# Column-group sums behind relu in late items, and first-pass evictions ahead of a conversion

## The chip, the cores and the metric

The kernel runs on one core of a Trainium2 chip. The time is the device time of one execution in microseconds (us); the median of three runs of the kernel before is 480.83 us (479.24 to 481.24). Engines as the profile names them: PE is TensorE (PEld its weight loads), DVE is VectorE, ACT is ScalarE, POOL is GpSimd, SP is SyncE, which issues the transfers.

## The reference

Three stages follow each other: chunked attention with memory tokens, a soft mixture of experts, and a squared-relu feed-forward layer. The change lies in the last:

```
h = x @ w_in            # x: 3072 x 512, w_in: 512 x 2048
r = np.maximum(h, 0.0)
g = s * (r * r) + b
out = g @ w_out         # w_out: 2048 x 512
```

Here x is itself `c @ slot_out`, with c of 32 columns (one per slot), so that h = c @ (slot_out @ w_in). The kernel forms m = slot_out @ w_in first, and h from c and m with one matmul for each block.

## The kernel before

The last stage cuts the 3072 tokens into 8 blocks of 384, and the 2048 hidden columns into 16 blocks f of 128. One pair (token block, f) is an **item**. Items 0 to 15 are the first pass: token blocks 0 and 1 in turn, f from 0 to 7. Items 16 to 47 are the second: blocks 2 and 3 in turn, all 16 f. Then blocks 4 to 7 follow alone, and at the end blocks 0 and 1 for f from 8 to 15.

Work of one item n: a matmul of 384 columns into a bank of the PSUM pool "s", which has two banks (`emit_h`, line 825, tile s); on ScalarE relu (line 831), square (line 835) and a rounded copy ghi (line 839); on VectorE the rest glo = square - ghi (line 842). Three items later nine matmuls of 512 columns use them: ghi and glo with the high part of w_out (`emit_o`, line 877) and, an item later still, ghi with its low part (`emit_o2`, line 889). They add up in three banks for each token block: pt, x, xt for one, lp and two of g for the other. When the last f of a run is done, the three sums are scaled and evicted, two on VectorE (line 896), one on ScalarE (line 894). After the first pass, the first matmul of the second pass on the same three banks waits for that. Square has two buffers, so the square of item n needs glo of item n-2 to be done.

The weights arrive packed and are converted on the way, one block in every second item up to item 46: ScalarE scales (`stage_a`, line 579), VectorE takes steps 0 to 3 (`stage_d`: lines 589, 591, 593, 600), and for w_out ScalarE casts a high part (`stage_w`, line 798) and VectorE forms the low part (lines 791, 793). Items 0 to 14 and 32 to 46 convert w_out, items 16 to 30 the later columns of w_in. Packed blocks lie in a ring of three slots; SyncE refills a slot when its last conversion is done (line 212).

The matrix m is made in groups of 512 columns. Group 0 is made around the first items, outside this loop. Groups 1, 2 and 3 are made in items 4, 26 and 34 (`M_AT`), each in two steps: in item n eight matmuls (line 806), which leave partial sums in four groups of 32 partitions, and ScalarE's copy of them to the tile mps (line 808); in item n+1 two matmuls that add the four groups and spread the sum (line 812), ScalarE's copy of the result into mpack (line 817), and VectorE's rest for the lower half (line 818). Both steps take a bank of the pool "s". These are the sums over column groups of which the change speaks.

Nothing schedules the work: each engine runs its instructions in the order in which the loop over n writes them, and waits on semaphores for the others. So where `emit_m` and `emit_m2` stand in the loop sets where lines 808 and 817 stand in ScalarE's queue.

Of the kernel before, what the change touches and what calls it, by code (L numbers as in the profile page):

```python
# [35 lines left out]
def kernel(  # L36
# [30 lines left out]
    def psum(tag, shape):  # L67
        bufs = {"s": 2, "g": 2}.get(tag, 1)
        return ps.tile(shape, F32, tag=tag, name=tag, bufs=bufs)
# [48 lines left out]
    with tc.manual_schedule():  # L118
# [45 lines left out]
        NRG, E_AT = 3, 5  # L164
        EARLY = [("wi", 2), ("wi", 3)]
        order = [("w1", i) for i in range(W1)] + [("wi", 0), ("wi", 1)] + [("w2", i) for i in range(W2)]
# [4 lines left out]
        order = order[0:-E_AT] + EARLY + order[-E_AT:]  # L171
# [9 lines left out]
        last_use = {}  # L181
# [7 lines left out]
        wnext = [0]  # L189
# [382 lines left out]
        def wi_dst(t, key):  # L572
            j = key[2]
            return t[j % 2][:, :, 256 * (j // 2):256 * (j // 2) + 256]
# [6 lines left out]
        def cv_dve(key, j):  # L581
            h, lf, a, w = cv[key]
            H = w[:, :, 1]
            hi, ai = h.bitcast(I32), a.bitcast(I32)
            if key[0] == "i" and key[1] > 1 and j:
                ai = wi_dst(wis_b if key[1] % 2 else wis_a, key).bitcast(I32)
                hi, H = (x.rearrange("p (k f) -> p k f", k=2) for x in (hi, H))
            if j == 0:
                nc.vector.tensor_scalar(out=hi, in0=hi, scalar1=3, scalar2=None, op0=ALU.logical_shift_left)
            elif j == 1:  # L590
                nc.vector.scalar_tensor_tensor(out=ai, in0=H, scalar=SIGN, in1=hi, op0=ALU.bitwise_and, op1=ALU.bitwise_or)
            else:
                nc.vector.tensor_scalar(out=hi, in0=ai, scalar1=EXPM, scalar2=None, op0=ALU.bitwise_and)

        def cv_low(key, out):
            h, lf, a, w = cv[key]
            low = w[:, :, 0].bitcast(U32)
            if key[0] == "i":
                low, h = (x.rearrange("p (k f) -> p k f", k=2) for x in (low, h))
            nc.vector.scalar_tensor_tensor(out=out, in0=low, scalar=2.0 ** -52, in1=h, op0=ALU.mult, op1=ALU.mult)  # L600
# [145 lines left out]
        M_AT = (4, 26, 34)  # L746
# [14 lines left out]
        HF = NF // 2  # L761
# [20 lines left out]
        def stage_d(k, j):  # L782
            key = cq.get(k)
            if key:
                h, lf, a, w = cv[key]
                if j < 3:
                    cv_dve(key, j)
                elif j == 3:
                    cv_low(key, lf if key[0] == "o" else wi_dst([wis_l[:, 0:2], wis_l[:, 2:4]], key))
                elif key[0] == "o" and j == 4:  # L790
                    nc.vector.tensor_tensor(out=a, in0=a, in1=w_hi[key[1]].bitcast(F32), op=ALU.subtract)
                elif key[0] == "o":
                    nc.vector.tensor_tensor(out=w_lo[key[1]], in0=a, in1=lf, op=ALU.add)

        def stage_w(k):
            key = cq.get(k)
            if key and key[0] == "o":
                nc.scalar.copy(out=w_hi[key[1]], in_=cv[key][2])

        def emit_m(fb):  # L800
            wis = wis_b if fb % 2 else wis_a
            mp = psum("s", [128, 512])
            for lo in range(1 if fb == 1 else 2):
                for kc in range(KD):
                    lhsT, rhs = (soTb[:, kc, :], wis_l[:, kc, :]) if lo else (soT4[:, kc, 0, :], wis[kc // 2][:, kc % 2, :])
                    nc.tensor.matmul(out=mp[32 * kc:32 * kc + 32, :], lhsT=lhsT, rhs=rhs,
                                     start=(lo == 0), stop=(lo == 1 or fb == 1))
            nc.scalar.copy(out=mps, in_=mp)

        def emit_m2(fb):  # L810
            mr = psum("s", [128, 512])
            nc.tensor.matmul(out=mr, lhsT=stks_all, rhs=mps, start=True, stop=True)
            m_split(mr, 512 * fb, slice(0, 512))

        def m_split(mp, base, cols):
            m = mpack[:, base + cols.start:base + cols.stop]
            nc.scalar.copy(out=m, in_=mp[:, cols])
            nc.vector.tensor_tensor(out=m[64:128], in0=mp[64:128, cols], in1=m[64:128].bitcast(F32), op=ALU.subtract)  # L818

        def emit_h(n):  # L820
            if n >= len(items):
                return
            (b, _, _), f = items[n]
            hq = psum("s", [128, UT])
            nc.tensor.matmul(out=hq, lhsT=mpack[:, 128 * f:128 * f + 128], rhs=cpack[:, b * UT:(b + 1) * UT],  # L825
                             start=True, stop=True)
            h_t[n] = hq

        def emit_relu(n):
            if n < len(items):  # L830
                nc.scalar.activation(out=r_g[n % 2], in_=h_t.pop(n), func=AF.Relu)  # L831
# [5 lines left out]
        def emit_ghi(n):  # L837
            if n < len(items):
                nc.scalar.copy(out=ghi_g[n % (LA + 2)], in_=r2_g[n % 2])  # L839
# [15 lines left out]
        def store(b, t, os_):  # L855
            nc.sync.dma_start(out=out[b * UT + 128 * t:b * UT + 128 * t + 128, :], in_=os_)

        def os_early(b, t):
            return area(16 * SLOT + DM * (NTU * b + t), DM)
# [20 lines left out]
        def emit_o2(n):  # L880
            r_, f = items[n]
            b, f0, f1 = r_
            ghi, glo = ghi_g[n % (LA + 2)], glo_g[n % (LA + 2)]
            for t in range(NTU):
                o = o_t[r_][t]
                if n == len(items) - 1:
                    for gt in (ghi, glo):
                        nc.tensor.matmul(out=o, lhsT=gt[:, 128 * t:128 * t + 128], rhs=w_hi[f], start=False, stop=False)
                nc.tensor.matmul(out=o, lhsT=ghi[:, 128 * t:128 * t + 128], rhs=w_lo[f], start=False, stop=(f == f1 - 1))  # L889
                if f == f1 - 1:  # L890
                    if b < 4 and f0 == 0:
                        to = part[b][t] if b < 2 else os_early(b - 2, t)
                        if t == 1:
                            nc.scalar.activation(out=to, in_=o, func=AF.Copy, scale=sbt[:, 0:1])
                        else:
                            nc.vector.tensor_scalar(out=to, in0=o, scalar1=sbt[:, 0:1], scalar2=None, op0=ALU.mult)  # L896
                    else:
                        os_ = os_g[t]
                        nc.vector.scalar_tensor_tensor(out=os_, in0=o, scalar=sbt[:, 0:1], in1=part[b][t] if f0 else bias,
                                                       op0=ALU.mult, op1=ALU.add)  # L900
                        store(b, t, os_)
# [12 lines left out]
        def stages(n, *js):  # L914
            for j in js:
                stage_d(n, j)


        cp = (nc.scalar.copy, nc.vector.tensor_copy)
        sot = psum("g", [128, 2, 4, 32])  # L920
# [47 lines left out]
        for n in range(LA + 1, len(items) + LA + 1):  # L968
            if n > 7:
                emit_h(n)  # L970
            m = n - LA - 1
            ends = 0 <= m and items[m][1] == items[m][0][2] - 1
            late = m + 1 < len(items) and m + 1 == 2 * HF + 1
            if ends or late:
                emit_o2(m)
            if 1 < m + 1 < len(items):
                emit_o(m + 1)
            if m > 1 and not ends and not late:
                emit_o2(m)
            if LA + 1 < n <= 7:  # L980
                emit_h(n)
            if n == 6:
                nc.vector.tensor_copy(out=soTb, in_=soT4[:, :, 0, :])
            if n in M_AT:
                emit_m(M_AT.index(n) + 1)
            if n - 1 in M_AT:
                emit_m2(M_AT.index(n - 1) + 1)
            emit_relu(n)
            emit_sq(n)
            stage_a(n + 1)  # L990
            emit_ghi(n)
            if LA + 1 < n <= len(items):
                emit_g(n - 1)
            stage_d(n, 1)
            stage_w(n)
            stages(n, 2, 3)
            stages(n - 1, 4, 5)
            stage_d(n + 1, 0)
            if 48 <= n < 64:
                for i in (2 * n - 96, 2 * n - 95):  # L1000
                    wsum_add(i)
            if n == 64:
                colsum()
            if 65 <= n < 77:
                add_bias(n - 65)
            while wnext[0] < len(order) and last_use.get(order[wnext[0] - NRG], -1) <= n:
                load_w(1)


# [70 lines left out]
```

## Time and profile before

| | us |
|---|---|
| median of three runs | 480.83 (479.24 to 481.24) |
| profiled execution | 479.52 |
| its span | 477.7 |
| PE busy | 456.7 (96%) |
| DVE busy | 310.1 (65%) |
| ACT busy | 308.7 (65%) |
| POOL busy | 84.4 (18%) |
| DMA engines, share of the span (q1) | 44.6% |

Busy times are sums over the span; they say which engine is worked most, not what an edit in one stage is worth. The last stage starts at about 167 us, and the changed items lie between 204 and 290 us. The profile gives each wait by the engine and line that ended it; a matmul's busy time includes its way through the pipeline, so that matmuls in a row overlap in it.

### The profile page before, as it was taken

To read this page: it belongs to the slowest core of one execution; us is meant where nothing else is said; L and a number is where in the kernel's file an instruction comes from. 1 tells how busy PE (TensorE), PEld (TensorE's weight loads), DVE (VectorE), ACT (ScalarE), POOL (GpSimd) and SP (SyncE) were. 2 spreads that over 40 slices of the span, in tenths; PEclk is the share of its full clock that TensorE was granted. 3 is DMA by queue.
4 is the path that set the end of the run, shared out by engine and by line. 5 is a ranking of instruction groups with operands and counts; after the bars stand their busy time and mean duration, and the time that the engine had idled before them with its cause. 6 is when DMAs were issued, how large, how long until landed. Compare 5 with 4: busy or idle time off the path is not lost.

```text
span 477.7 us, 10206 instructions
## 1 busy us (share of the span) xinstructions
PE 456.7 (96%) x3960; PEld 342.3 (72%) x3960; DVE 310.1 (65%) x685; ACT 308.7 (65%) x635; POOL 84.4 (18%) x154
## 2 busy tenths in 40 slices
PE   7899998999999999999898999999999999999996
PEld 5666666665555467868585888888888888888885
DVE  6778887885485889997484999975524224223232
ACT  4566666675144388888576897666666666666660
POOL 6666665650000000000000000007700000000000
PEclk9999999999999999999999999999999999999999
DMA  8999999999999934234222000003101001001011
GB/s 304 385 406 405 406 409 398 397 381 396 401 420 392 414 128 151 89 99 166 88 89 88 1 1 0 1 0 146 55 0 67 0 1 67 0 1 66 1 67 66
DMA packets 20576, 83.04 MB, mean 174 GB/s; under 512 B 2736, under 2 KB 2864, under 8 KB 14640
## 3 DMA queue, kind: packets, MB, share of 16 engines
q1 hardware_dynamic: 20528, 82.39, 44.6%
q8 instruction: 31, 0.51, 0.4%
q14 instruction: 17, 0.14, 0.1%
HBM read 76.09 MB, written 6.29 MB: 172 GB/s over the span
## 4 chain that ended last, share of the span: by engine, by line
PE 69%; DVE 13%; DMA 8%; ACT 4%; issue 3%; SPq 2%; POOL 1%; DVEq 0%; POOLq 0%; ACTq 0%
PE g L877 11%; PE lp L877 5%; PE pt L877 5%; PE x L877 5%; PE g L889 5%; PE xt L877 5%; PE s L825 4%; DMA seg<-in_w_dram 4%; PE s L630 3%; PE x L325 3%; DMA vals<-in_vm_dram 3%; PE lp L889 3%; PE pt L889 3%; PE xt L889 3%; PE x L889 3%
## 5 line engine op out<-in xcount | busy, mean ns | idle before, releaser
L842 DVE TENSOR_TENSOR glo<-r,ghi 128x384 fp32r<-128x384 f32 x128 | 76.3, 601 | 81.6 <-ACT ghi L839 81.4
L831 ACT ACTIVATE r<-s 128x384 f32<-128x384 f32 x128 | 62.8, 491 | 52.8 <-PE s L825 52.4
L835 ACT ACTIVATE r<-r 128x384 f32<-128x384 f32 x128 | 67.4, 527 | 6.2 <-DVE glo L842 2.0
L839 ACT CAST ghi<-r 128x384 fp32r<-128x384 f32 x128 | 65.7, 513 | 3.4
L825 PE MATMUL s<-cpack,mpack 128*128 128x384 f32 x128 | 44.2, 348 | 3.7 <-ACT r L831 2.1
L301 ACT ACTIVATE seg<-seg 128x384 f32<-128x384 f32 x32 | 28.8, 900 | 19.2 <-DVE seg L312 15.1
L889 PE MATMUL g<-wlo,ghi 128*128 128x512 f32 x128 | 40.2, 394 | 0.0
L877 PE MATMUL g<-whi,ghi 128*128 128x512 f32 x126 | 39.7, 394 | 0.2 <-DVE mpack L818 0.2
L877 PE MATMUL g<-whi,glo 128*128 128x512 f32 x126 | 39.3, 393 | 0.0
L864 POOL TENSOR_TENSOR keys<-keys,bias 128x512 f32<-128x512 f32 x6 | 8.4, 1426 | 168.7 <-DVE bias L853 168.7
L263 POOL TENSOR_SCALAR keys<-keys 64x416 f32<-64x416 f32 x63 | 33.7, 536 | 12.7 <-DMA keys<-in_kq_dram 7.5
L285 PE MATMUL s<-keys 128*32 128x128 f32 x768 | 30.3, 291 | 4.4 <-POOL keys L267 3.4
L825 PEld LDWEIGHTS s<-cpack,mpack 128*128 128x128 f32 x128 | 23.9, 188 | 13.0 <-ACT r L831 4.4
L325 PE MATMUL x<-vals,seg 128*32 128x128 f32 x744 | 28.0, 275 | 2.8 <-DMA vals<-in_vm_dram 2.0
L325 PEld LDWEIGHTS x<-vals,seg 128*32 128x32 f32 x744 | 20.3, 109 | 13.2 <-DVE seg L309 6.4
L889 PEld LDWEIGHTS g<-wlo,ghi 128*128 128x128 f32 x128 | 24.0, 188 | 5.3
L877 PEld LDWEIGHTS g<-whi,glo 128*128 128x128 f32 x126 | 23.7, 188 | 5.3
L285 PEld LDWEIGHTS s<-keys 128*32 128x32 f32 x768 | 19.5, 113 | 10.4 <-POOL keys L267 6.0
L319 ACT COPY seg<-pt 128x384 f32<-128x384 f32 x32 | 15.3, 478 | 17.9 <-PE pt L317 16.9
L877 PEld LDWEIGHTS g<-whi,ghi 128*128 128x128 f32 x126 | 23.7, 188 | 4.3 <-DVE mpack L818 0.7
L877 PE MATMUL lp<-whi,ghi 128*128 128x512 f32 x63 | 25.5, 404 | 0.9 <-DVE vals L896 0.9
L877 PE MATMUL pt<-whi,ghi 128*128 128x512 f32 x64 | 25.6, 400 | 0.0
(255 smaller groups left out, 991.1 us busy)
## 6 DMA issues: line engine op xcount, KB each, us to landing
seg<-in_w_dram SPq DMA_DIRECT2D x27, 1024.0 KB, 8.5
keys<-in_kq_dram SPq DMA_DIRECT2D x32, 396.0 KB, 7.4
vals<-in_vm_dram SPq DMA_DIRECT2D x64, 192.0 KB, 6.5
keys<-in_w_in_dram SPq DMA_DIRECT2D x5, 1024.0 KB, 5.1
keys<-in_w_out_dram SPq DMA_DIRECT2D x5, 1024.0 KB, 4.9
out_dram<-os SPq DMA_DIRECT2D x18, 256.0 KB, 2.1
vals<-in_w_in_dram SPq DMA_DIRECT2D x3, 1024.0 KB, 5.6
vals<-in_w_out_dram SPq DMA_DIRECT2D x3, 1024.0 KB, 4.9
```

The costliest lines, as they stand in the source:

```text
L263: (nc.vector if h and u == 0 else nc.gpsimd).tensor_scalar(out=stream(kz[rows, h], 0, CH), in0=k[rows, UT * h:UT * h + (NCU + 1) * CH].rea ...
L285: nc.tensor.matmul(out=o, lhsT=qt[:, 32 * c:32 * c + 32], rhs=kz[:, :, at:at + WIN], start=True, stop=not (first or last))
L301: nc.scalar.activation(out=p_r[u], in_=sm_r[u].rearrange("p t h (a r) -> p t r (h a)", a=2), func=AF.Exp, scale=scale)
L319: nc.scalar.copy(out=pts_r[u], in_=pt)
L325: nc.tensor.matmul(out=xp[32 * r:32 * r + 32, t], lhsT=pts_r[u][:, 32 * c:32 * c + 32], rhs=vbuf[u // 2 % 2][:, u % 2, :, 64 * c:64 * c + ...
L825: nc.tensor.matmul(out=hq, lhsT=mpack[:, 128 * f:128 * f + 128], rhs=cpack[:, b * UT:(b + 1) * UT], start=True, stop=True)
L831: nc.scalar.activation(out=r_g[n % 2], in_=h_t.pop(n), func=AF.Relu)
L835: nc.scalar.activation(out=r2_g[n % 2], in_=r_g[n % 2], func=AF.Square)
L839: nc.scalar.copy(out=ghi_g[n % (LA + 2)], in_=r2_g[n % 2])
L842: nc.vector.tensor_tensor(out=glo_g[n % (LA + 2)], in0=r2_g[n % 2], in1=ghi_g[n % (LA + 2)].bitcast(F32), op=ALU.subtract)
L877: nc.tensor.matmul(out=o_t[r_][t], lhsT=gt[:, 128 * t:128 * t + 128], rhs=w_hi[f], start=(f == r_[1] and gt is ghi), stop=False)
L889: nc.tensor.matmul(out=o, lhsT=ghi[:, 128 * t:128 * t + 128], rhs=w_lo[f], start=False, stop=(f == f1 - 1))
```

## The change

Two edits in the loop over n, and nothing else; no instruction is added or removed.

The two steps of a column group (`sums`) stand ahead of relu only in items up to 7, that is, for group 1. For groups 2 and 3 (items 26, 27, 34 and 35) they stand behind relu, square, the scaling of the next weight block and ghi, still ahead of glo of the item before.

The conversion steps of item 18 (`convert`, from step 1 on) and the refill that depends on them are written in item 19, behind the evictions of item 15 (the second token block of the first pass).

```
+        def sums(n):
+            if n in M_AT:
+                emit_m(M_AT.index(n) + 1)
+            if n - 1 in M_AT:
+                emit_m2(M_AT.index(n - 1) + 1)
+
+        def convert(n):
+            stage_d(n, 1)
+            stage_w(n)
+            stages(n, 2, 3)
+            stages(n - 1, 4, 5)
+            stage_d(n + 1, 0)
...
             if ends or late:
                 emit_o2(m)
+            if n == 2 * HF + 3:
+                convert(n - 1)
             if 1 < m + 1 < len(items):
                 emit_o(m + 1)
...
-            if n in M_AT:
-                emit_m(M_AT.index(n) + 1)
-            if n - 1 in M_AT:
-                emit_m2(M_AT.index(n - 1) + 1)
+            if n <= 7:
+                sums(n)
             emit_relu(n)
             emit_sq(n)
             stage_a(n + 1)
             emit_ghi(n)
+            if n > 7:
+                sums(n)
             if LA + 1 < n <= len(items):
                 emit_g(n - 1)
-            stage_d(n, 1)
-            stage_w(n)
-            stages(n, 2, 3)
-            stages(n - 1, 4, 5)
-            stage_d(n + 1, 0)
+
+            if n != 2 * HF + 2:
+                convert(n)
...
-            while wnext[0] < len(order) and last_use.get(order[wnext[0] - NRG], -1) <= n:
+            while n != 2 * HF + 2 and wnext[0] < len(order) and last_use.get(order[wnext[0] - NRG], -1) <= n:
                 load_w(1)
```

HF is 8, so the two numbers are 18 and 19. On ScalarE, at items 26 and 27 (rows with + are new, with - gone; r and ghi are item 26's, then item 27's):

```order
+L831 ACTIVATE r_2658<-s 128x384
+L835 ACTIVATE r_2660<-r_2658 128x384
+L839 CAST ghi_2663<-r_2660 128x384
 L808 COPY mps_2657<-s 128x512
-L831 ACTIVATE r_2658<-s 128x384
-L835 ACTIVATE r_2660<-r_2658 128x384
-L839 CAST ghi_2663<-r_2660 128x384
+L831 ACTIVATE r_2659<-s 128x384
+L835 ACTIVATE r_2661<-r_2659 128x384
+L579 ACTIVATE seg_99<-keys 128x512
+L839 CAST ghi_2664<-r_2661 128x384
 L817 CAST mpack<-s 128x512
```

The copy to mps now follows item 26's three activations, and the copy into mpack follows item 27's four; at items 34 and 35 it is the same, with one cast of line 798 between the copy to mps and item 35's relu. TensorE's order is the same in both kernels.

On VectorE, at the end of the first pass (glo of item 17, the conversion of item 18, the evictions of item 15, glo of item 18):

```order
 L842 TENSOR_TENSOR glo_2669<-r_2661,ghi_2664 128x384
+L896 TENSOR_SCALAR vals_104<-lp,cstt 128x512
+L896 TENSOR_SCALAR vals_104<-g,cstt 128x512
 L591 SCALAR_TENSOR_TENSOR seg_99<-keys 128x2x256
 L593 TENSOR_SCALAR keys<-seg_99 128x512
 L600 SCALAR_TENSOR_TENSOR seg_101<-keys 128x2x256
-L896 TENSOR_SCALAR vals_104<-lp,cstt 128x512
-L896 TENSOR_SCALAR vals_104<-g,cstt 128x512
 L842 TENSOR_TENSOR glo_2670<-r_2660,ghi_2665 128x384
```

The two evictions now stand ahead of the three conversion steps; glo of item 18 stays behind all five.

## Rows read from the trace of the kernel before

**Rows 1.** Busy time by stretch: us, PE, PEld, DVE, ACT, POOL, PEclk, DMA share, GB/s.

```profile
230.00:240.00 10.00, 8.25 (x40) 5.85 (x33) 5.10 (x9) 7.34 (x16) 0.00 (x0) 1.00 0.31 105
...
260.00:270.00 10.00, 10.00 (x46) 8.29 (x45) 9.79 (x20) 8.76 (x18) 0.00 (x0) 1.00 0.01 2
```

**Rows 2.** Waits from 205 to 330 us: engine, line, releaser; total, times, longest us.

```profile
PE s L825 <- ACT r L831: 2.1, 2, 1.1
...
PE s L825 <- ACT mps L808: 1.4, 2, 0.7
...
PE lp L877 <- DVE vals L896: 0.9, 1, 0.9
...
PEld s L825 <- ACT mps L808: 2.8, 2, 1.4
```

**Rows 3.** Timeline, items 26 to 30: start, us, engine, instruction, [idle before, releaser].

```profile
226.85 0.34 PE L825 MATMUL s<-cpack,mpack 128*128 128x384 f32 x1
...
230.08 0.40 PE L806 MATMUL s<-seg 128*32 128x512 bf16 x4
230.52 0.59 ACT L808 COPY mps<-s 128x512 f32<-128x512 f32 x1 [3.54 <-PE s L806]
...
231.16 0.45 PE L825 MATMUL s<-cpack,mpack 128*128 128x384 f32 x1 [0.68 <-ACT mps L808]
...
233.50 1.02 PE L812 MATMUL s<-mps,stk 128*128 128x512 f32 x2
234.56 0.59 ACT L817 CAST mpack<-s 128x512 fp32r<-128x512 f32 x1 [1.96 <-PE s L812]
...
235.18 0.69 DVE L818 TENSOR_TENSOR mpack<-s,mpack 64x512 fp32r<-64x512 f32 x1 [3.97 <-ACT mpack L817]
...
235.91 0.56 DVE L842 TENSOR_TENSOR glo<-r,ghi 128x384 fp32r<-128x384 f32 x1
...
237.94 0.34 PE L825 MATMUL s<-cpack,mpack 128*128 128x384 f32 x1
...
238.81 0.39 PE L877 MATMUL pt<-whi,glo 128*128 128x512 f32 x1
...
240.20 0.34 PE L825 MATMUL s<-cpack,mpack 128*128 128x384 f32 x1
```

**Rows 4.** Timeline: the hidden-layer matmuls of items 34 and 37.

```profile
249.24 0.34 PE L825 MATMUL s<-cpack,mpack 128*128 128x384 f32 x1
...
260.35 0.34 PE L825 MATMUL s<-cpack,mpack 128*128 128x384 f32 x1
```

**Rows 5.** Timeline at the end of the first pass, items 18 to 21.

```profile
209.65 0.63 PE L889 MATMUL g<-wlo,ghi 128*128 128x512 f32 x2
...
211.28 0.69 DVE L591 SCALAR_TENSOR_TENSOR seg<-keys 128x512 int32<-128x512 int32 x1
...
211.98 0.34 PE L825 MATMUL s<-cpack,mpack 128*128 128x384 f32 x1
...
213.07 0.75 DVE L896 TENSOR_SCALAR vals<-lp,cstt 128x512 f32<-128x512 f32 x1
...
214.38 0.55 DVE L842 TENSOR_TENSOR glo<-r,ghi 128x384 fp32r<-128x384 f32 x1
...
215.56 0.34 PE L825 MATMUL s<-cpack,mpack 128*128 128x384 f32 x1
...
216.43 0.40 PE L877 MATMUL pt<-whi,glo 128*128 128x512 f32 x1
```

**Rows 6.** Timeline: glo of items 36 and 38 on VectorE.

```profile
262.72 0.55 DVE L842 TENSOR_TENSOR glo<-r,ghi 128x384 fp32r<-128x384 f32 x1
...
267.12 0.55 DVE L842 TENSOR_TENSOR glo<-r,ghi 128x384 fp32r<-128x384 f32 x1
```

**Rows 7.** SyncE's issues of w_in (timeline), and time to landing (page part 6).

```profile
204.32 9.22 SPq L212 DMA_DIRECT2D keys<-in_w_in_dram  x2
...
keys<-in_w_in_dram SPq DMA_DIRECT2D x5, 1024.0 KB, 5.1
```

## The prediction

> **What bounds the kernel now.** I read the busy table by stretches first. In most of the last stage TensorE has no idle time (10.00 us of 10 in 260 to 270), while 230 to 240 shows 8.25; its clock is granted in full in both [rows 1]. So the last stage is paced by matmuls except at a few holes, and only a hole can be won. The list of waits names them: twice 0.7 us until ScalarE's copy of the column-group sums (line 808), twice 1.1 us until a relu, and 0.9 us until a VectorE eviction (line 896) [rows 2]. No other wait of a matmul between 205 and 330 us is in that list. Then I read the timeline at each hole, and there the reader sees the queue rather than the work: ScalarE stood idle for 3.54 us before the copy at 230.52, because the copy needs the eight matmuls that end at 230.48, and item 26's relu, whose matmul started at 226.85, stood behind it [rows 3].
>
> **Sums behind ghi, items 26 and 34.** Nothing is added or removed; on ScalarE two copies change places with relu, square and ghi of the same item. The price before, first place: from item 26's hidden-layer matmul at 226.85 to that of item 29 at 237.94 are 11.09 us, against 3 x 2.26 = 6.78 for three steady items (237.94 to 240.20 is one) [rows 3]. After: relu, square and ghi of item 26 fit in the 3.54 us that ScalarE was idle, so item 27's matmul no longer waits for the copy. It starts when the eight matmuls end (230.48; they start the steady item's end, 226.85 + 2.26 = 229.11, so they cost 1.37). Its first successors then run as before, up to the regrouping matmuls 2.34 us later (231.16 to 233.50, less 0.11 for the restart below: 2.23, so 232.71). Their input, the copy, is there: ScalarE is free, and starts it at 230.52 as before, done by 231.11. These two matmuls take 1.02, to 233.73. Item 28's matmul needs item 27's relu, which now stands in front of the second copy: it starts after the first copy, about 231.0, and is done by 231.5. So no hole is left: 6.78 + 1.37 + 1.02 = 9.17, and 11.09 - 9.17 = 1.92. Matmuls that follow without a wait overlap a little (two in a row are busy 0.63 together where one is 0.40 [rows 5]), which adds up to 0.17 at each of the two holes: at most 2.26. The least is the two idle times alone, 0.7 + 1.1 = 1.8 [rows 2]. I take 2.0, near the upper end, since it rests on whole items. The second place has the same length, 249.24 to 260.35 = 11.11 [rows 4], so another 2.0.
>
> What is late next: the second copy starts when the regrouping ends, 233.73 + 0.04, not at 234.56. VectorE's split of it (line 818) keeps its old place, ahead of glo of item 26, and starts 0.62 after the copy: 234.4; glo follows 0.73 later and ends at about 235.7 [rows 3]. TensorE reads that glo at 238.81 before, at 236.8 after: the margin falls from 2.34 to 1.1 us, but stays. Square of item 28 waits for the same glo (they share a buffer), so ScalarE is idle for about a microsecond there; the relu of item 28 is ahead of that and done by 234.8, and item 29's matmul, which now waits for it (it gets its bank), comes at 236.0. So nothing reaches TensorE.
>
> **A restart, weighed with the skill.** The weight load of that matmul waited too, 2.8 us at two places [rows 2], and the matmul after a wait is busy 0.45 us where the steady one takes 0.34 [rows 3]; each hole therefore costs about 0.11 beyond its idle time, and that comes back with it. The Trainium skill (TensorE: Matmul & The Clock Gate, Engine queue depths) says that TensorE's queue can pull a weight load ahead of matmuls in flight. By that rule no restart would be paid, and the sum below would be 0.11 x 5 = about 0.5 us smaller (476.2); the trace shows the load held up along with its matmul, so I keep the row's price.
>
> **Evictions ahead of item 18's conversion.** On VectorE, three conversion steps (lines 591, 593, 600) and two evictions of 128x512 change places. Their sum is unchanged: the steps take 213.07 - 211.28 = 1.79, the evictions 214.38 - 213.07 = 1.31, and glo of item 18 still starts at 214.38 [rows 5]. The evicted sums were complete at 209.65 + 0.63 = 210.28, so the evictions can start at 211.28 and free their banks by 212.7. The items around it are 211.98 to 215.56 = 3.58 apart instead of 2.26: TensorE gets 1.32 at most, and at least the 0.85 to 0.9 of pure idle time [rows 2, 5]. One thing eats into this: glo of item 18 ends at 214.93 as before, and TensorE, now 1.32 earlier, wants it at 215.1 instead of 216.43 [rows 5]; that leaves 0.17, and the weight load, which is what reads glo, comes before its matmul. I take 0.2 off: 1.1. The later conversion delays the load of the ring slot that it frees (SyncE's queue) by 1.3 us: the second issue of the pair, 204.32 + 9.22 - 0.33 = 213.2, becomes 214.5; landing takes 5.1, so 219.6, and its first reader, ScalarE's scaling for item 28, stands behind item 27's relu, which starts at about 231.0 [rows 7]. SyncE has nothing else queued in between that an earlier item needs. GpSimd is not touched.
>
> **Sum.** 2.0 + 2.0 + 1.1 = 5.1 us, all on TensorE's path, after which the remaining items only start earlier. The profiled execution took 479.52 (span 477.7, 1.8 around it, which no edit touches): 474.4. The median of the three runs is 480.83, 1.3 above, so I forecast 480.83 - 5.1 = 475.7. From the bounds: 1.8 + 1.8 + 0.85 = 4.5 to 2.26 + 2.26 + 1.32 = 5.8.
>
> **Rivals.**
> The wait moves instead of going: the split of the second copy blocks VectorE, and glo of items 26 and 34 comes after TensorE wants it. For it: glo then comes 1.2 us later relative to TensorE, and the margin falls to 1.1 us. Against: 1.1 us is over half of the whole chain copy, split, glo. If each place gives back what its relu wait cost, 1.07: 480.83 - 5.1 + 2.1 = 477.8. The Trainium skill (the same section) calls VectorE's queue a strict FIFO; by that nothing behind the split can pass it, as the rows show it for glo.
>
> The gain is absorbed later, by VectorE in the second pass. From item 36 on it is 97.9% busy (9.79 of 10) [rows 1] and needs 267.12 - 262.72 = 4.40 us for a pair of items [rows 6], where TensorE needs 4.52. After the change it enters that stretch 1.2 us later relative to TensorE. For it: only 0.12 us per pair to spare. Against: it is still the quicker of the two, so the lag shrinks, and 2.34 - 1.2 of margin are left. To absorb all of 5.1 us, six pairs would have to be 1.0 us longer than TensorE's: 480.8.
>
> Slower: the same stretch, items 36 to 47, if ScalarE and VectorE come into step. ScalarE's cast of the high weights waits for line 591 on VectorE, VectorE's subtraction waits for the cast; with less lead each pair could lose a wait on both sides. It decides from 4.52 + (5.1 + 2.4 + 1.1) / 6 = 5.95 us a pair on; at 6.2 the six pairs lose 10.1, less 1.1 of margin and 5.1 of gain: 480.83 + 3.9 = 484.7. Against: the pair takes 4.40 with those waits already in it.
>
> **How the numbers follow.** Forecast 0.75, moved wait 0.12, absorbed 0.08, slower 0.05. 0.5% is 2.4 us, about what a measurement can tell from no change. The forecast is faster; of the moved wait most; so faster 0.83, same 0.12, slower 0.05. Range: the forecast's own is 480.83 - 5.8 to 480.83 - 4.5, widened by the spread of the runs shown (479.24 to 481.24): 473.4 to 476.8. To take in the moved wait with its part ways, the upper end goes to 478.3.
>
> **What would show it.** In the list of waits the entries of line 825 on lines 808 and 831 are gone, and so is the one on line 896; three items around each sum take about 9.1 us instead of 11.1, and the two items around the first pass's end 2.3 to 2.5 instead of 3.58. ScalarE's idle time before line 808 falls from 3.5 to about 1.8 us, and VectorE still waits some 2 to 5 us before line 818. I am wrong if TensorE waits for glo within four items after either sum, or if VectorE's margin reaches zero before item 47.

## The result and the profile after

The changed kernel takes 474.97 us (median of six runs, 473.61 to 476.14), the kernel before in the same series 480.39 (479.24 to 481.32). The ratio is 0.9884, with a 95% interval of 0.9858 to 0.9909: 5.6 us less, between 4.4 and 6.8. The forecast was 475.7.

The waits between 205 and 325 us after the change (engine, line, releaser; total, times, longest us) hold no entry for a TensorE matmul any more; what stands for these lines now is this:

```profile
DVE mpack L818 <- ACT mpack L817: 8.3, 2, 5.1
ACT r L835 <- DVE glo L842: 3.8, 5, 1.1
ACT mps L808 <- PE s L806: 3.4, 2, 1.7
...
PEld pt L877 <- DVE glo L842: 0.2, 1, 0.2
```

The three matmul waits of [rows 2] are gone. In the list before, two rows for ScalarE read:

```profile
ACT mps L808 <- PE s L806: 7.1, 2, 3.5
...
ACT r L835 <- DVE glo L842: 1.0, 1, 1.0
```

So ScalarE waits 3.4 us before its copy at two places where it waited 7.1, and 3.8 us for glo instead of 1.0: the waiting has moved to engines that have time. Busy time by stretch, columns as in [rows 1]:

```profile
230.00:240.00 10.00, 10.00 (x48) 7.56 (x41) 6.04 (x12) 7.38 (x16) 0.00 (x0) 1.00 0.30 105
260.00:270.00 10.00, 10.00 (x46) 8.25 (x45) 9.76 (x20) 9.08 (x19) 0.00 (x0) 1.00 0.00 1
```

The hole of 1.75 us between 230 and 240 is closed. The timeline of items 26 to 30, which answers to [rows 3]:

```profile
227.00 0.34 PE L825 MATMUL s<-cpack,mpack 128*128 128x384 f32 x1
...
227.37 0.49 ACT L831 ACTIVATE r<-s 128x384 f32<-128x384 f32 x1 [0.25 <-PE s L825]
...
230.56 0.44 PE L825 MATMUL s<-cpack,mpack 128*128 128x384 f32 x1
...
230.67 0.59 ACT L808 COPY mps<-s 128x512 f32<-128x512 f32 x1 [1.70 <-PE s L806]
...
231.15 0.50 ACT L831 ACTIVATE r<-s 128x384 f32<-128x384 f32 x1
...
232.90 1.02 PE L812 MATMUL s<-mps,stk 128*128 128x512 f32 x2
...
233.95 0.59 ACT L817 CAST mpack<-s 128x512 fp32r<-128x512 f32 x1 [0.79 <-PE s L812]
...
234.57 0.69 DVE L818 TENSOR_TENSOR mpack<-s,mpack 64x512 fp32r<-64x512 f32 x1 [3.21 <-ACT mpack L817]
...
235.28 0.56 DVE L842 TENSOR_TENSOR glo<-r,ghi 128x384 fp32r<-128x384 f32 x1
...
236.02 0.33 PE L825 MATMUL s<-cpack,mpack 128*128 128x384 f32 x1
...
236.88 0.40 PE L877 MATMUL pt<-whi,glo 128*128 128x512 f32 x1
```

Item 26's relu starts 0.37 us after its matmul, at 227.37; before, it was 4.15 (226.85 to 231.00 in the trace). From item 26's matmul to item 29's are 236.02 - 227.00 = 9.02 us, where [rows 3] has 11.09. The price stands in the two rows of VectorE: glo ends at 235.84, and TensorE's first matmul with it starts at 236.88, a margin of 1.04 us instead of 2.34 (its weight load, which is what reads glo, starts at 236.66). The second place, as [rows 4]: 256.32 - 247.30 = 9.02 instead of 11.11.

```profile
247.30 0.34 PE L825 MATMUL s<-cpack,mpack 128*128 128x384 f32 x1
...
256.32 0.33 PE L825 MATMUL s<-cpack,mpack 128*128 128x384 f32 x1
```

The end of the first pass, as [rows 5]:

```profile
212.78 0.74 DVE L896 TENSOR_SCALAR vals<-lp,cstt 128x512 f32<-128x512 f32 x1
...
213.48 0.34 PE L825 MATMUL s<-cpack,mpack 128*128 128x384 f32 x1
...
214.10 0.68 DVE L591 SCALAR_TENSOR_TENSOR seg<-keys 128x512 int32<-128x512 int32 x1
...
215.73 0.34 PE L825 MATMUL s<-cpack,mpack 128*128 128x384 f32 x1
...
215.88 0.55 DVE L842 TENSOR_TENSOR glo<-r,ghi 128x384 fp32r<-128x384 f32 x1
...
216.60 0.39 PE L877 MATMUL pt<-whi,glo 128*128 128x512 f32 x1
```

The eviction now stands ahead of line 591, and the two items are 2.25 us apart instead of 3.58. Glo of item 18 ends at 216.43 and is read at 216.60: 0.17 us of margin, and its weight load waited 0.2 us (the last row of the waits), but the matmul came on its beat. In the second pass, as [rows 6], with TensorE's reading of item 36:

```profile
260.00 0.55 DVE L842 TENSOR_TENSOR glo<-r,ghi 128x384 fp32r<-128x384 f32 x1
...
261.69 0.39 PE L877 MATMUL pt<-whi,glo 128*128 128x512 f32 x1
...
264.39 0.55 DVE L842 TENSOR_TENSOR glo<-r,ghi 128x384 fp32r<-128x384 f32 x1
```

A pair takes VectorE 4.39 us, and the margin is 1.14 us at item 36; it grows to 1.78 at item 46, and no matmul waits.

The three distances together give 2.07 + 2.09 + 1.33 = 5.49 us. The two profiled executions differ by less, 479.52 - 475.50 = 4.02. The rest is not the change's: in the profiled execution of the changed kernel the last stage begins 1.48 us later (its first matmul with glo at 172.58 instead of 171.10). At the first matmul of line 668, in the stage before, this execution was not behind yet (141.84 instead of 141.92). The delay comes from two waits after it, both behind a transfer. In the kernel before:

```profile
164.25 0.64 PE L668 MATMUL xt<-seg,seg 128*32 128x256 f32 x8 [0.34 <-DMA seg<-in_w_dram]
...
167.39 0.67 ACT L579 ACTIVATE seg<-keys 128x512 f32<-128x512 f32 x1
...
170.33 0.47 PE L877 MATMUL pt<-whi,ghi 128*128 128x512 f32 x1
```

In the changed kernel:

```profile
164.90 0.64 PE L668 MATMUL xt<-seg,seg 128*32 128x256 f32 x8 [0.79 <-DMA seg<-in_w_dram]
...
168.88 0.67 ACT L579 ACTIVATE seg<-keys 128x512 f32<-128x512 f32 x1 [0.74 <-DMA keys<-in_w_out_dram]
...
171.81 0.47 PE L877 MATMUL pt<-whi,ghi 128*128 128x512 f32 x1 [0.78 <-DVE whi L953]
```

The matmuls of line 668 end up 0.65 us later, waiting for weights. Then ScalarE waits 0.74 us for the packed w_out, and the first matmul with w_out waits 0.78 us for its high part, made from that. Neither wait is in an order that the change touches.

### The profile page after: what moved, and what is told of

It is laid out like the page before. It is cut to its first block, busy times and chain, and to the rows that moved or that the text cites. A ratio compares the mean times of both kernels' runs of the same rounds, so it can differ in the third digit from the quotient of the medians.

```text
span 473.7 us, 10205 instructions
## 1 busy us (share of the span) xinstructions
PE 454.6 (96%) x3960; PEld 342.4 (72%) x3960; DVE 309.3 (65%) x685; ACT 307.4 (65%) x635; POOL 84.2 (18%) x154
## 4 chain that ended last, share of the span: by engine, by line
PE 73%; DMA 10%; DVE 9%; ACT 3%; POOL 2%; issue 1%; SPq 1%; DVEq 0%; POOLq 0%; ACTq 0%
PE g L877 12%; PE pt L877 6%; PE x L877 6%; PE xt L877 6%; PE lp L877 6%; PE g L889 6%; PE s L825 5%; DMA keys<-in_w_out_dram 4%; PE s L630 3%; PE pt L889 3%; PE xt L889 3%; PE lp L889 3%; PE x L889 3%; DMA keys<-in_kq_dram 3%; PE x L325 2%; PE s L285 2%
## 5 line engine op out<-in xcount | busy, mean ns | idle before, releaser
L889 PE MATMUL pt<-wlo,ghi 128*128 128x512 f32 x64 | 25.4, 396 | 0.2 <-DVE wlo L793 0.2
```

## The experiments

All edits are against the changed kernel, all ratios against the kernel before, run beside it. The distances between hidden-layer matmuls (line 825) are read from each kernel's timeline and sum all that happens between; they repeat within some 0.04 us, where the medians of the two series of the changed kernel (after and e10) are 0.5 apart.

| kernel | median us | ratio, 95% | items 19-20 | 20-21 | 21-26 | 26-29 | 34-37 |
|---|---|---|---|---|---|---|---|
| before | 480.39 | | 2.74 | 3.58 | 11.29 | 11.09 | 11.11 |
| changed | 474.97 | 0.9884 (0.9858 to 0.9909) | 2.74 | 2.25 | 11.27 | 9.02 | 9.02 |
| e1 sums only | 476.14 | 0.9917 (0.9899 to 0.9935) | 2.70 | 3.57 | 11.28 | 9.02 | 9.02 |
| e2 evictions only | 479.02 | 0.9981 (0.9967 to 0.9995) | 2.72 | 2.24 | 11.28 | 11.12 | 11.11 |
| e3 sums in all items | 477.05 | 0.9933 (0.9915 to 0.9952) | 2.71 | 2.24 | 11.28 | 9.02 | 9.02 |
| e4 first step only | 478.15 | 0.9959 (0.9941 to 0.9976) | 2.70 | 2.24 | 11.29 | 10.34 | 10.33 |
| e5 glo first | 474.60 | 0.9875 (0.9857 to 0.9893) | 2.72 | 2.24 | 11.30 | 9.02 | 9.02 |
| e6 one addition | 475.27 | 0.9881 (0.9859 to 0.9903) | 2.70 | 2.24 | 11.30 | 9.01 | 9.01 |
| e7 three additions | 476.52 | 0.9924 (0.9903 to 0.9945) | 2.71 | 2.24 | 11.30 | 9.02 | 9.02 |
| e8 scaling step too | 474.31 | 0.9866 (0.9848 to 0.9884) | 2.35 | 2.24 | 11.63 | 9.02 | 9.02 |
| e9 conversion last | 474.38 | 0.9880 (0.9861 to 0.9900) | 2.39 | 2.25 | 11.30 | 9.01 | 9.01 |
| e10 changed again | 474.46 | 0.9882 (0.9862 to 0.9903) | 2.74 | 2.24 | 11.30 | 9.02 | 9.02 |

**Each part alone (e1, e2).** In e1 the conversion goes back, in e2 the sums:

```
# e1
-            if n == 2 * HF + 3:
-                convert(n - 1)
-            if n != 2 * HF + 2:
-                convert(n)
+            convert(n)
# e2
-            if n <= 7:
-                sums(n)
+            sums(n)
             emit_relu(n)
...
-            if n > 7:
-                sums(n)
```

> The sums of items 26 and 34 behind ghi as in the changed kernel, but item 18's conversion back in item 18, ahead of the evictions. Queue theory (each hole closes by itself and the gains add up): hidden-layer matmuls of items 26 to 29 and 34 to 37 are 9.0 us apart as in the changed kernel, those of items 20 and 21 3.6 as in the kernel before; the time falls by 2.07 + 2.09 = 4.2 us against before (476.2). Rival (the gains hang together: TensorE that is earlier after the first pass makes ScalarE and VectorE late at item 26): the holes close by less than 2.0 each, or by more.

> Item 18's conversion behind the evictions as in the changed kernel, but all column-group sums ahead of relu. Queue theory: items 20 and 21 are 2.25 us apart instead of 3.58, the two places of the sums stay at 11.1; the time falls by 1.3 us against before (479.1). Rival (the 1.3 us are only handed on: TensorE arrives earlier at the waits at item 26, where ScalarE holds it): items 26 to 29 get longer than 11.1 and the time falls by under 0.5.

Both came out as the queue theory has them: 476.14 and 479.02, with each distance at one of its two values and nothing between. The list of waits of e1 holds the one that its part leaves:

```profile
PE lp L877 <- DVE vals L896: 0.9, 1, 0.9
```

So the two parts add up (0.83% and 0.19%, together 1.02% of the 1.16%, within the intervals), and neither hands its gain on to the other.

**The two steps of the sums apart (e4).**

```
-            if n > 7:
-                sums(n)
+            if n > 7 and n in M_AT:
+                emit_m(M_AT.index(n) + 1)
```

with `emit_m2` of items 27 and 35 ahead of relu.

> The changed kernel with only the first step of the sums (eight matmuls, copy to mps) behind ghi in items 26 and 34; the second step (regrouping, copy into mpack, split) stays ahead of relu in items 27 and 35. It tells the two holes at each place apart. Queue theory: the first hole closes (0.7 to 0.8 us), the second (1.3 to 1.4 us with its restart) stays, since relu of items 27 and 35 still stands behind the second copy: items 26 to 29 are 10.35 us apart, the time is 2.7 us above the changed kernel (477.7). Rival (the first hole caused the second one): both close, 9.0 and the time of the changed kernel.

The distances are 10.34 and 10.33, so the first step is worth 0.76 and the second 1.32 at each place; the wait that stays is the second one:

```profile
PE s L825 <- ACT r L831: 2.1, 2, 1.1
```

The holes do not cause each other. The median, 478.15, is 0.45 above what was expected, within its interval.

**Where the move does not pay (e3).** The condition on n is gone, and the sums of items 4 and 5 stand behind ghi too.

> The changed kernel with the sums of item 4 and 5 behind ghi as well. Queue theory (the move pays only where ScalarE was idle ahead of the copy and glo has margin): at item 4 ScalarE had no idle time before the copy and glo of item 4 was 0.1 us ahead of TensorE, so the later copy holds up the regrouping matmuls by about 1 us and the split holds up glo by about 0.7 to 1 more: 1.5 to 2 us slower than the changed kernel (476.5 to 477). Rival (behind ghi is the better place in every item, since relu is what TensorE waits for): as fast as the changed kernel or up to 1 us faster.

It is slower than the changed kernel, 477.05, and the timeline shows why at items 4 to 7: the regrouping matmuls waited 0.82 us for the copy, which before had its turn in time, and glo, behind the split, came 0.73 us late.

```profile
179.72 1.12 PE L812 MATMUL s<-mps,stk 128*128 128x512 f32 x2 [0.82 <-ACT mps L808]
...
183.19 0.69 DVE L818 TENSOR_TENSOR mpack<-s,mpack 64x512 fp32r<-64x512 f32 x1 [1.89 <-ACT mpack L817]
...
184.51 0.50 PE L877 MATMUL pt<-whi,glo 128*128 128x512 f32 x1 [0.73 <-DVE glo L842]
```

The two waits are 1.55 us, and items 4 to 9 are 12.76 us apart instead of 10.87. So it is not the place behind ghi that is better, but ScalarE's idle time ahead of the copy and VectorE's margin: where neither is there, the same move costs 1.9 us.

**The margin at glo (e5, e6, e7).** In e5 glo of the item before is written ahead of the sums; in e6 and e7 one and three additions are put between the split and glo at both places:

```
             if n > 7:
                 sums(n)
+            if n > 7 and n - 1 in M_AT:
+                for _ in range(3):
+                    nc.vector.tensor_tensor(out=wsum, in0=w_hi[0].bitcast(F32), in1=w_lo[0].bitcast(F32), op=ALU.add)
```

> The changed kernel with glo of the item before written ahead of the sums in items 26, 27, 34 and 35, so that on VectorE glo no longer stands behind the split. Queue theory (the margin of 1.0 us at glo is not used up, so a larger one is worth nothing): the margin of glo of items 26 and 34 grows to over 3 us, ScalarE's idle time before square of items 28 and 36 goes, items 26 to 29 stay 9.0 us apart, the time is that of the changed kernel within 0.5 us. Rival (VectorE's lag of 1.2 us in the second pass costs TensorE something later): 0.5 to 1.5 us faster than the changed kernel.

> The changed kernel with one extra addition of 128x512 (0.73 us from start to start in the trace of before) on VectorE between the split and glo of items 26 and 34; its result is overwritten later. Queue theory: 0.73 is within the margin of 1.0 us, the margin falls to 0.3, TensorE waits nowhere: the time of the changed kernel within 0.5 us. Rival (VectorE sets the pace of the second pass): 0.7 us at each place, 1.5 us slower.

> As the one with one extra addition, with three: 2.2 us more on VectorE ahead of glo of items 26 and 34. Queue theory: 2.2 - 1.04 = 1.15 us beyond the margin at each place, with a restart of up to 0.3: TensorE waits for glo at both places, 2.3 to 2.9 us slower than the changed kernel. If VectorE set the pace: 2 x 2.2 = 4.4 us slower. If the margins are larger than read: no change.

In e6 glo starts 1.31 us behind the split, where it was 0.71 (234.57 to 235.28 in the changed kernel):

```profile
234.97 0.69 DVE L818 TENSOR_TENSOR mpack<-s,mpack 64x512 fp32r<-64x512 f32 x1 [3.21 <-ACT mpack L817]
...
236.28 0.55 DVE L842 TENSOR_TENSOR glo<-r,ghi 128x384 fp32r<-128x384 f32 x1
```

So one addition takes 0.60 us out of the margin, not the 0.73 that was reckoned, and 0.45 are left. With the margin at item 26 raised to 5.06 us (e5) and with 0.60 us taken out of it (e6), all distances and the time stay (474.60 and 475.27 beside 474.46 and 474.97). With three additions TensorE waits at both places (the waits of e7, and its timeline at item 26's glo):

```profile
PE pt L877 <- DVE glo L842: 1.8, 2, 0.9
```

```profile
232.97 0.69 DVE L818 TENSOR_TENSOR mpack<-s,mpack 64x512 fp32r<-64x512 f32 x1 [3.21 <-ACT mpack L817]
...
235.74 0.55 DVE L842 TENSOR_TENSOR glo<-r,ghi 128x384 fp32r<-128x384 f32 x1
...
236.35 0.50 PE L877 MATMUL pt<-whi,glo 128*128 128x512 f32 x1 [0.90 <-DVE glo L842]
```

Glo starts 2.77 us behind the split, 2.06 later than in the changed kernel (2.2 were reckoned). Items 29 to 34 are 12.45 us apart instead of 11.28, so these 2.06 us cost 1.17. Beyond the margin stand 2.06 - 1.04 = 1.02; 0.06 pass from glo's end at 236.29 to the matmul, and the matmul is busy 0.50 us after its wait instead of 0.40, a restart of 0.10. VectorE does not set the pace of the second pass, and the margin is what the rows say. By the median e7 is 1.6 to 2.1 us above the two series of the changed kernel, less than the 2.3 that were the low end of what was expected; the two places in the timeline give 2.3 to 2.4.

**Further on (e8, e9).** One hole is left in this stretch: 2.74 us between items 19 and 20. In e8 step 0 of item 18's conversion stands behind item 14's evictions (and glo first, as in e5); in e9 the other steps stand behind glo of item 18 as well:

```
# e8, in convert and in the loop
+            if n != 2 * HF + 1:
                 stage_d(n + 1, 0)
...
             if n != 2 * HF + 2:
                 convert(n)
+            else:
+                stage_d(n, 0)
# e9: e8, with convert(n - 1) of n == 2 * HF + 3 at the end of the item
```

> The changed kernel with glo ahead of the sums (as in the kernel of that name) and with step 0 of item 18's conversion (line 589) behind the evictions of item 14 as well. Queue theory: the last hole in this stretch, 2.74 us between the hidden-layer matmuls of items 19 and 20 instead of 2.26, closes, since the eviction of pt starts 0.46 us earlier: 0.4 to 0.5 us faster than the changed kernel (474.5), which the median can hardly show but the distance of the two matmuls does. Rival (the eviction then waits for TensorE's own sums): 2.74 stays.

> As the kernel with step 0 of item 18's conversion behind item 14's evictions and glo ahead of the sums, but with the rest of item 18's conversion behind glo of item 18 too. In the kernel without this, the 0.4 us won at items 19 and 20 came back as a wait of 0.51 us of TensorE's weight load for glo of item 18. Queue theory: glo of item 18 now starts 1.8 us earlier, that wait goes, and the 0.4 us stay: items 19 and 20 2.35 us apart, items 21 to 26 11.28, 0.4 us faster than the changed kernel (474.5). Rival (the conversion that is later still makes another glo or the sums of item 26 late): items 21 to 26 stay at 11.6 or get longer.

e8 wins 0.39 us at items 19 and 20 and loses 0.35 at items 21 to 26. This loss was not expected: of the 0.4 to 0.5 us, 0.04 are left. TensorE arrives there earlier than glo of item 18, whose margin of 0.17 us was all there was; its weight load waits:

```profile
214.56 0.55 DVE L842 TENSOR_TENSOR glo<-r,ghi 128x384 fp32r<-128x384 f32 x1
...
215.17 0.19 PEld L877 LDWEIGHTS pt<-whi,glo 128*128 128x128 f32 x1 [0.51 <-DVE glo L842]
```

In e9 that wait is gone and the gain stays: 2.39 and 11.30. By the distances e9 is 0.35 us faster than the changed kernel; the medians (474.38 beside 474.46 on the same chip) cannot tell the two apart.

> The changed kernel once more, unaltered, beside the others on the same chip: 475.0 us, ratio 0.988 to before, items 19 and 20 2.74 us apart, 20 and 21 2.25, 21 to 26 11.27.

The repeat agrees: 0.9882 beside 0.9884.

## Why the prediction was right

The sum was 5.1 us, and the distances give 5.49; the ratio says 5.6 (4.4 to 6.8). Point by point:

- **The holes, and what made them.** Queue position, as forecast: relu starts when its matmul is done, and e4 shows that each hole belongs to its own copy.
- **The size at each place**, 2.0: 2.07 and 2.09. The pieces were each a little off and in part cancel, which is luck: from item 26 to 27 3.56 us (3.63 reckoned), on to the regrouping matmuls 2.34 (2.23), on to item 29 3.12 (3.31), together 9.02 instead of 9.17. The first hole gave 0.76, its idle time of 0.68 and almost nothing more, since item 27's matmul is still busy 0.44 us although it waits for nothing; the second gave 1.32, its 1.07 and 0.25 more. So the 0.11 for a restart was not one price: behind the small matmuls of the sums it is paid with or without a wait, while e7's wait for glo shows it at 0.10. What the 0.25 consist of was not taken apart. The Trainium skill's rule that weight loads can be pulled ahead of matmuls in flight (TensorE: Matmul & The Clock Gate, Engine queue depths), taken to hold across a wait as the prediction weighed it, would have made the gain smaller. The distances do not bear that reading out, since together both holes gave 0.33 beyond their idle time.
- **Glo's margin**, forecast 1.1: 1.04 and 1.02. That it is enough was the step on which the first rival hung, and e6 and e7 show that it ends between 0.60 and 2.06 us of delay.
- **Evictions**, 1.1: 1.33. Here a term was mis-sized: the 0.2 us taken off for glo of item 18. The margin was 0.17 as worked out, but the load's wait of 0.2 us lay beside other matmuls and cost nothing: the two items are as close (2.25) as steady ones. e8 shows that the concern was only 0.4 us too early: there the same wait reaches TensorE.
- **The second pass**, the rivals "absorbed" and "slower": VectorE took 4.39 us a pair against TensorE's 4.52, as before, and the lag shrank. Nothing was absorbed.
- **The time.** 475.7 rested on the three runs shown before (480.83); six runs have 480.39. Those 0.44 us are chance, in the direction of the miss; with the 0.4 that the sum was short they cover the difference of 0.73 to 474.97.

## What to carry to other kernels

An instruction that waits, at the head of an engine's queue, costs what stands behind it: look for idle time of an engine that is not the bound just before an instruction on which the bound does not yet depend, and move the ready work ahead of it. Before moving, read two margins from the trace: the idle time ahead of the moved instruction, and how early its consumers' data now come; what is moved ahead is free as long as it fits into the first (in e3, without such idle time, the copy made TensorE wait 0.82 us), and the delay of the others is free as long as it stays within the second (e6 and e7). Judge edits worth a few tenths of a microsecond by the distance between two marks in the trace, since medians of whole runs vary by more.

## What was not expected of the hardware

The profiled execution of the changed kernel had a granted clock of 0.51 from 10 to 15 us, and that of the kernel before 1.00, in a stretch that the change does not touch (columns as in [rows 1]):

```profile
10.00:15.00 5.00, 5.00 (x65) 3.13 (x57) 2.99 (x9) 2.34 (x4) 2.34 (x6) 0.51 0.98 366
```

That is nearly the lower of the two levels (1.2 of 2.4 GHz), after a stretch from 5 to 10 us in which TensorE was busy 1.98 of 5 us; over its first 25 us this execution has a mean of 0.86. It is tempting to put the 1.48 us by which its last stage begins later down to the clock. The traces speak against it: at the first matmul of line 668 the execution was 0.08 us ahead of the kernel before (141.84 instead of 141.92), and the delay arose behind that. In e3 the clock was 0.55 from 10 to 15 us, and its first hidden-layer matmul starts at 167.84, where the kernel before has 167.87; in e2 it was 1.00 over the first 25 us, and that matmul starts at 170.04. So the low clock at this place cost no time that the start of the last stage shows. Why the transfers of the weights land at different times was not tried, nor what brought the clock down in one execution and not in the other; the mean granted clock of the profiled executions goes from 0.988 to 1.000 over the kernels of this study, which all begin alike.
